# Attention and a gated feed-forward layer on one core: another table for the order of the steps and for the places of their tiles

## The chip, the core and the metric

The kernel runs on one core of a Trainium2 chip. The metric is the time of one execution on the device in microseconds (us), the median of several runs. Engines: PE is TensorE (its weight loads, PEld, run beside its matmuls), DVE is VectorE, ACT is ScalarE, POOL is GpSimd; SP issues nearly all transfers. Each engine works through its own queue in the written order and waits, where it must, for semaphores of other engines and of transfers.

## The reference

```python
k_all = concat([k_g, k_l]); v_all = concat([v_g, v_l])          # 8 batches, 8 heads, 32 + 512 rows, 64 columns
out_g = softmax(q_g @ k_all.T / 8) @ v_all                      # 32 global rows see all
s_l   = concat([q_l @ k_g.T, where(|i - j| <= 32, q_l @ k_l.T, -1e9)]) / 8
out_l = softmax(s_l) @ v_all                                    # 512 local rows see a band and the global rows
x  = concat([out_g, out_l]) as 4352 tokens x 512
xn = x / sqrt(mean(x * x) + 1e-6) * rms_g
g  = xn @ w_gate; v = xn @ w_val                                # 512 x 1536 each
y  = (g * sigmoid(g) * v) @ w_out                               # 1536 x 512
```

## The kernel before

The tokens come in nine chunks: chunk c of 0 to 7 holds the 512 local rows of batch c, chunk 8 the 256 global rows of all batches. While the feed-forward products of chunk c run, the attention of chunk c + 1 or c + 2 is done in pieces between them. Weights and tokens are split into a high and a low part in float16, and a product is three matmuls.

All steps are first only written down, under names, and then issued in the order of a table. `ORDER` (line 66) lists 3692 names as `chunk:step.part`; each engine's queue is what the list has for it, in the list's order, so moving a name moves all its instructions, transfers too. `PAGES` (line 391) gives each of 1169 larger tiles, in the order in which they are written down, one of 43 pages of 4 KB per partition (`a` to `d` are its quarters) or of 8 wider ones; `BANKS` (line 438) gives 444 PSUM tiles one of 8 banks. A tile that gets a place which another one had waits for that one's last reader. `JOBS` (line 40), which holds the steps of the first stage in their logical order, and all code stand as they are. The issuing loop is the last of the kernel:

```python
for name in ORDER.split() or list(plan):
    for call in plan.pop(name):
        call()
```

The first stage (the names that begin with `0:`) makes chunk 0's attention in four units of two heads (0 to 3) and chunk 1's in units 4 to 7, readies the weights, and does the feed-forward of chunk 0. Its steps, for a unit u:

- `Lu` loads queries and keys (256 and 384 KB), `Su` is 32 score products on PE (64 instructions), `Mu.h.g` adds the mask and takes the row's extreme on DVE (four for a half h), `Eu.h` is four exponentials on ACT, `Tu.h` four transposes on PE, `Cu.h` their copy out of PSUM on ACT, `Vu` loads the values (1 MB), `Au` is the product with them on PE (64 instructions), `Ru` and `Xu` divide on DVE, `Qu` squares on ACT and `Zu` sums on DVE.
- For a weight block i: `Wi` loads 1 MB, `mi`, `si`, `li` or `ki`, `gi` make it float32 (m and k on ACT, or m and l on DVE; s and g on DVE), `qi` sums squares on ACT, `ai` (ACT) and `di` (DVE) split it. `pg` sums a group's squares on PE and `eg` makes its scales on DVE. `z0` to `z6` handle the norm's gains.
- `N0.0` to `N0.12` are small DVE steps for the norm of chunk 0, `D0.j` its four diagonal matrices, `U0.k` the turn on PE (8 instructions each), `H0.k` (ACT) and `Y0.k` (DVE) the high and low parts.
- `If.wi` are the first feed-forward products of chunk 0 (6 matmuls of 512 columns), `B`, `b`, `h`, `c`, `r` what follows on ACT and DVE, `Oi.j` the second products.

From chunk 1 on, `c:Pk` and `c:Ok` are steps of a chunk's products, `c:Rk`, `c:tk`, `c:nk` what DVE, ACT and POOL do on them, `c:wk` transfers of weights, and `c:X/i+d` the attention steps of chunk c + d: `S` (scores, 128 PE instructions), `A` and `B` (values, 80 each), `GS`, `GT`, `GA` for the global rows.

Of the kernel before, what the change touches and what calls it, by code (L numbers as in the profile page):

```python
# [2327 lines left out]
```

## Time and profile before

| | us |
|---|---|
| median of 3 runs | 902.93 |
| lowest and highest | 902.28, 904.0 |
| the profiled execution | 904.84 |
| its span, first to last instruction | 903.1 |
| PE busy in the span | 869.2 |

The span is what the profile resolves; the profiled execution took 1.7 us more than it. PE is the busiest engine. A busy PE counts a matmul's pipelined end too, so beside the busy time the idle time in front of its instructions is to be read, with what ended it, and the TensorE clock that was granted.

### The profile page before, as it was taken

The page shows a single profiled execution, that of the slowest core. Times are in us where ns is not written, and L with a number is a line of the kernel's source. Part 1 is how long each engine was busy: PE and PEld are TensorE (multiplying, and loading weights), DVE is VectorE, ACT ScalarE, POOL GpSimd, SP SyncE. Part 2 cuts the span into 40 slices and gives each one's busy share as a digit, 9 for nine tenths or more (in the row PEclk, how much of TensorE's full clock was granted, in tenths as well). Part 3 has the DMA queues.
Part 4 walks back from the last instruction along what each step waited for, and adds up shares of the span by engine and source line. Part 5 has one row for each costly group of instructions (what it writes and reads, how often), then busy time and mean ns, then how long its engine had stood idle before and what let it go on. Part 6 is the DMA issues. An engine that isn't in the chain of part 4 may idle for free. (4 is left out here: it accounts for less than half of the span.)

```text
span 903.1 us, 27864 instructions
## 1 busy us (share of the span) xinstructions
PE 869.2 (96%) x11430; PEld 668.4 (74%) x11430; DVE 701.2 (78%) x1831; ACT 553.8 (61%) x1341; POOL 273.8 (30%) x244
## 2 busy tenths in 40 slices
...
DMA packets 101007, 212.04 MB, mean 235 GB/s; under 512 B 8080, under 2 KB 34448, under 8 KB 100880
## 3 DMA queue, kind: packets, MB, share of 16 engines
q1 hardware_dynamic: 100448, 209.94, 69.0%
q8 instruction: 89, 1.46, 0.7%
q10 hardware_dynamic: 432, 0.33, 0.1%
...
## 5 line engine op out<-in xcount | busy, mean ns | idle before, releaser
L2088 PE MATMUL bank<-page,page 128*128 128x256 f16 (+6 forms) x8212 | 714.6, 281 | 24.8 <-DMA page<-in_qk_dram 8.6
L2088 PEld LDWEIGHTS <-page 128*128 128x128 f16 (+1 forms) x5472 | 525.0, 98 | 175.5 <-issue 11.4
L2088 POOL TENSOR_TENSOR page<-page,page 128x512 f16<-128x512 f32 (+5 forms) x177 | 200.5, 1152 | 361.4 <-ACT page L2088 319.8
L2088 ACT CAST page<-page 128x512 f16<-128x512 f32 (+1 forms) x156 | 121.2, 797 | 93.4 <-DVE page L2088 72.5
L2088 ACT COPY page<-bank 128x512 f32<-128x512 f32 (+3 forms) x163 | 85.1, 543 | 115.7 <-PE bank L2088 103.1
L2088 DVE TENSOR_TENSOR page<-bank,page 128x512 f32<-128x512 f32 x155 | 104.7, 685 | 59.2 <-PE bank L2088 48.7
L2088 ACT ACTIVATE page<-page,sm 128x128 f32<-128x128 f32 x352 | 128.8, 389 | 24.4 <-DVE sm L2088 21.7
L2088 DVE TENSOR_TENSOR page<-page,page 128x256 f32<-128x256 f32 (+5 forms) x171 | 102.4, 609 | 11.0 <-ACT page L2088 8.7
L2088 PE MATMUL bank<-wide,page 32*64 32x96 f32 (+6 forms) x2268 | 103.5, 271 | 1.3 <-issue 1.3
L2088 POOL TENSOR_TENSOR page<-page,sm 128x512 f32<-128x512 f32 x24 | 27.9, 1176 | 214.4 <-DVE sm L2088 200.5
L2088 ACT ACTIVATE page<-page 128x512 f32<-128x512 f32 (+2 forms) x94 | 77.6, 894 | 10.2 <-DVE page L2088 5.5
L2088 PEld LDWEIGHTS bank<-page,page 64*32 64x32 f32 (+4 forms) x3232 | 58.4, 116 | 29.5 <-issue 14.7
L2088 DVE CUSTOM_DVE_ANT_0 page<-bank,page 128x128 f32<-128x128 f32 x256 | 62.0, 284 | 19.9 <-PE bank L2088 16.5
L2088 DVE TENSOR_TENSOR page<-page 128x256 f32<-128x256 f32 (+3 forms) x127 | 69.3, 556 | 1.2
L2088 DVE SCALAR_TENSOR_TENSOR page<-page,page 128x512 f32<-128x512 f32 x65 | 46.9, 734 | 12.6 <-ACT page L2088 12.4
L2088 DVE SCALAR_TENSOR_TENSOR page<-page,c_h,page 128x512 f32<-128x512 f32 x69 | 51.7, 769 | 0.9
L2088 ACT ACTIVATE page<-page,half_inv 128x512 f32<-128x512 f32 x65 | 44.6, 716 | 12.8 <-DVE page L2088 11.5
L2088 ACT ACTIVATION_READ_ACCUMULATOR page<-page,sm 128x1 f32 x256 | 48.0, 187 | 0.0
L2088 PE MATMUL bank<-page,wide 128*128 128x256 f16 x330 | 41.7, 273 | 0.6 <-ACT page L2088 0.6
L2088 ACT ACTIVATE page<-bank,half_inv 128x512 f32<-128x512 f32 (+1 forms) x36 | 21.7, 610 | 31.7 <-PE bank L2088 31.7
L2088 DVE STREAM_TRANSPOSE wide<-page 128x512 f32<-128x512 f32 x48 | 32.6, 696 | 6.5 <-POOL page L2088 6.5
L2088 PEld LDWEIGHTS <-wide 128*128 128x128 f16 x330 | 31.9, 98 | 5.1 <-issue 1.0
...
## 6 DMA issues: line engine op xcount, KB each, us to landing
page<-wd SPq DMA_DIRECT2D x113, 512.0 KB, 6.6
page<-wb SPq DMA_DIRECT2D x34, 512.0 KB, 7.2
page<-in_w_in_dram SPq DMA_DIRECT2D x24, 512.0 KB, 9.2
...
page<-wa SPq DMA_DIRECT2D x19, 512.0 KB, 6.0
...
page<-in_vw_dram SPq DMA_DIRECT2D x16, 512.0 KB, 8.9
```

Source lines behind the costliest of these rows:

```text
L2088: return lambda *a, **k: write(self.engine, lambda: call(*a, **k))
```

## The change

All three tables are replaced, `ORDER`, `PAGES` and `BANKS`; nothing else is. The names in `ORDER` are the same 3692, 118 of them at the same place in the list; 84 of 1169 pages and 57 of 444 banks are the same. No instruction is added or taken away. In the first stage the loads of units 0 and 1 come earlier (`L0` first, `L1` ahead of the weights), `T0` and the other steps of unit 0 come ahead of unit 2's, `E1` comes ahead of some of the work on weight blocks, and a step of `g2` stands between the `N0` and the `D0` steps. Later the changes are local: products of a chunk change places with each other and with the attention steps between them. The start of each table, and two later places of `ORDER`:

```diff
--- before
+++ after
 ORDER = """
-0:L2.0 0:L0.0 0:S0.0 0:M0.0.0 0:M0.0.3 0:M0.0.1 0:M0.0.2 0:E0.0.0 0:z0.0 0:M0.1.2 0:L3.0 0:W1.0
-0:W3.0 0:M0.1.3 0:M0.1.0 0:M0.1.1 0:S2.0 0:E0.1.0 0:M2.0.2 0:M2.1.1 0:M2.1.2 0:M2.0.0 0:L1.0
-0:M2.0.1 0:S3.0 0:M2.1.0 0:M2.0.3 0:M2.1.3 0:E2.1.0 0:E2.0.0 0:V0.0 0:z1.0 0:z2.0 0:M3.1.0 0:W0.0
-0:z2.1 0:z2.4 0:z2.5 0:M3.0.0 0:M3.0.1 0:z2.6 0:z3.0 0:M3.1.1 0:M3.1.3 0:M3.1.2 0:E3.1.0 0:M3.0.3
-0:m3.0 0:z4.1 0:M3.0.2 0:m1.1 0:m3.1 0:z2.2 0:T2.1.0 0:C2.1.0 0:T0.0.0 0:C0.0.0 0:z4.0 0:s3.0 0:z2.3
-0:E3.0.0 0:m1.0 0:T0.1.0 0:C0.1.0 0:T2.0.0 0:l1.1 0:s1.0 0:l1.0 0:S1.0 0:M1.0.0 0:M1.0.1 0:M1.0.2
-0:M1.0.3 0:E1.0.0 0:M1.1.3 0:M1.1.2 0:M1.1.0 0:M1.1.1 0:E1.1.0 0:g1.0 0:g1.1 0:V2.0 0:q1.0 0:V1.0
-0:R0.0 0:T3.1.0 0:V3.0 0:C2.0.0 0:T3.0.0 0:W2.0 0:A0.0 0:W4.0 0:m0.0 0:T1.0.0 0:T1.1.0 0:C3.0.0
-0:k3.0 0:L4.0 0:z4.2 0:m0.1 0:C3.1.0 0:l0.0 0:s0.0 0:C1.0.0 0:C1.1.0 0:X0.0 0:g0.0 0:W7.0 0:Q0.0
-0:A2.0 0:p1.0 0:l0.1 0:g0.1 0:q0.0 0:g3.0 0:g3.1 0:W5.0 0:R2.0 0:W8.0 0:X2.0 0:R3.0 0:e1.0 0:z5.0
-0:q3.0 0:z6.0 0:z6.1 0:z6.2 0:e1.1 0:A1.0 0:R1.0 0:X1.0 0:Q2.0 0:p0.0 0:e0.0 0:e1.2 0:e0.1 0:e0.3
-0:W6.0 0:Z2.0 0:e1.3 0:Q1.0 0:e0.2 0:A3.0 0:X3.0 0:a0.0 0:Z1.0 0:Q3.0 0:Z0.0 0:Z3.0 0:N0.0.0
-0:N0.1.0 0:N0.2.0 0:e0.4 0:N0.3.0 0:N0.4.0 0:N0.5.0 0:N0.6.0 0:N0.7.0 0:N0.8.0 0:N0.9.0 0:N0.10.0
-0:N0.11.0 0:N0.12.0 0:m2.0 0:s2.0 0:L5.0 0:D0.3 0:D0.2 0:k2.0 0:D0.1 0:D0.0 0:d0.0 0:m4.0 0:g2.1
-0:a1.0 0:U0.0.0 0:s4.0 0:U0.1.0 0:g2.0 0:W9.0 0:k4.0 0:m7.0 0:W11.0 0:H0.0.0 0:d1.0 0:g4.0 0:U0.3.0
-0:U0.2.0 0:Y0.0.0 0:q2.0 0:p2.0 0:H0.1.0 0:Y0.1.0 0:S4.0 0:H0.2.0 0:H0.3.0 0:e2.0 0:Y0.2.0 0:M4.0.0
...
+0:L0.0 0:S0.0 0:L2.0 0:S2.0 0:M0.0.2 0:M0.0.0 0:M0.0.1 0:z0.0 0:M0.0.3 0:M0.1.0 0:E0.0.0 0:M2.1.0
+0:M2.1.1 0:M2.1.2 0:M2.1.3 0:M0.1.2 0:L3.0 0:M2.0.2 0:E2.1.0 0:M0.1.1 0:M0.1.3 0:S3.0 0:M3.1.2
+0:z1.0 0:z2.0 0:M2.0.1 0:E0.1.0 0:M2.0.3 0:M2.0.0 0:E2.0.0 0:M3.0.3 0:M3.0.2 0:z2.1 0:M3.1.1
+0:M3.1.0 0:M3.1.3 0:E3.1.0 0:T0.0.0 0:C0.0.0 0:L1.0 0:M3.0.1 0:M3.0.0 0:E3.0.0 0:W1.0 0:V0.0 0:z2.4
+0:W0.0 0:m1.0 0:T0.1.0 0:T2.0.0 0:W3.0 0:z2.6 0:z2.5 0:l1.0 0:C2.0.0 0:m1.1 0:T2.1.0 0:C0.1.0 0:s1.0
+0:l1.1 0:g1.0 0:g1.1 0:q1.0 0:z3.0 0:z4.1 0:T3.1.0 0:z4.0 0:R0.0 0:S1.0 0:M1.0.3 0:M1.0.1 0:M1.0.0
+0:M1.0.2 0:V2.0 0:M1.1.1 0:M1.1.0 0:C2.1.0 0:M1.1.2 0:E1.0.0 0:M1.1.3 0:z4.2 0:R2.0 0:z2.2 0:m0.0
+0:m0.1 0:s0.0 0:A0.0 0:l0.0 0:m3.0 0:E1.1.0 0:g0.0 0:m3.1 0:k3.0 0:l0.1 0:T1.1.0 0:V1.0 0:T1.0.0
+0:p1.0 0:A2.0 0:s3.0 0:X0.0 0:g3.0 0:C1.0.0 0:Q0.0 0:g0.1 0:q0.0 0:T3.0.0 0:C1.1.0 0:g3.1 0:V3.0
+0:X2.0 0:z2.3 0:p0.0 0:e0.0 0:e0.1 0:e0.2 0:z5.0 0:C3.0.0 0:Q2.0 0:z6.0 0:W2.0 0:C3.1.0 0:e1.0
+0:q3.0 0:R3.0 0:A1.0 0:R1.0 0:Z0.0 0:e1.1 0:z6.1 0:W4.0 0:Z2.0 0:z6.2 0:X1.0 0:A3.0 0:a0.0 0:X3.0
+0:Q1.0 0:e1.2 0:L4.0 0:Z1.0 0:Q3.0 0:Z3.0 0:N0.0.0 0:N0.1.0 0:N0.2.0 0:N0.3.0 0:N0.4.0 0:N0.5.0
+0:N0.6.0 0:m2.0 0:s2.0 0:N0.7.0 0:k2.0 0:N0.8.0 0:N0.9.0 0:N0.10.0 0:N0.11.0 0:N0.12.0 0:g2.0 0:D0.1
+0:W7.0 0:a1.0 0:D0.2 0:D0.3 0:m4.0 0:W5.0 0:W6.0 0:D0.0 0:U0.3.0 0:U0.0.0 0:d0.0 0:g2.1 0:e0.3
+0:s4.0 0:U0.1.0 0:k4.0 0:d1.0 0:g4.0 0:q2.0 0:H0.1.0 0:U0.2.0 0:H0.0.0 0:g4.1 0:m7.1 0:S4.0 0:m5.0
+0:k5.0 0:Y0.1.0 0:q4.0 0:Y0.0.0 0:H0.3.0 0:e1.3 0:p2.0 0:m7.0 0:H0.2.0 0:M4.0.0 0:e2.0 0:M4.0.2
+0:e2.1 0:a2.0 0:m6.0 0:s7.0 0:s5.0 0:e0.4 0:g5.1 0:e2.3 0:k6.0 0:L5.0 0:g5.0 0:q5.0 0:Y0.3.0
+0:Y0.2.0 0:e0.5 0:W8.0 0:e1.4 0:l7.0 0:W12.0 0:I0.00.0 0:I1.00.0 0:l7.1 0:g7.0 0:g7.1 0:q7.0 0:m8.0
+0:W11.0 0:I0.10.0 0:d2.0 0:I1.10.0 0:a3.0 0:M4.1.3 0:I0.11.0 0:s6.0 0:I0.01.0 0:M4.1.2 0:I1.11.0
+0:g6.0 0:I1.01.0 0:g6.1 0:M4.1.1 0:p3.0 0:q6.0 0:B0.0 0:e3.0 0:m11.0 0:I2.00.0 0:W9.0 0:e2.4
+0:I2.01.0 0:l8.1 0:M4.0.3 0:e2.2 0:W10.0 0:B1.0 0:M4.1.0 0:e3.3 0:m9.0 0:M4.0.1 0:W17.0 0:e2.5
...
-2:P48.0 2:P49.0 2:P50.0 2:t37.1 2:t42.1 1:GX/1+1.1 2:w41.0 2:Y/2+1.1 2:t38.1 2:R41.2 2:t43.1
-2:S/0+2.0 2:P46.0 2:t44.0 2:X/2+1.3 2:t43.0 2:M1/0+2.1 2:t43.2 2:t44.1 2:N1/0+2.0 2:Y/2+1.2 2:P51.0
...
+2:w41.0 2:GX/1+1.0 2:GX/1+1.1 2:R41.2 2:t42.0 2:P49.0 2:X/2+1.0 1:R53.1 2:t42.1 2:t36.1 2:t43.0
+3:w13.0 2:t43.1 2:X/2+1.2 2:w44.0 2:P50.0 2:P51.0 2:t37.1 2:t38.1 2:t44.0 2:t45.0 2:X/2+1.3 2:P52.0
+2:Y/2+1.0 2:Y/2+1.2 2:P46.0 2:S/0+2.0 2:Y/2+1.3 2:n45.0 2:n45.1 2:M1/0+2.1 2:M0/0+2.0 2:N3/0+2.0
...
-5:R34.0 5:t35.0 5:t36.0 5:R34.1 5:t35.1 5:t36.1 5:w36.0 5:t19.0 5:P37.0 5:P38.0 5:B/2+1.0 5:w40.0
...
+5:P37.0 5:t35.1 5:R36.1 5:t36.0 5:t36.1 5:R36.0 5:P39.0 5:R39.0 5:B/2+1.0 5:V/0+2.0 5:O1.0 5:t37.0
...
 PAGES = """
-3a 0c 2a 0c 3c 10a 2a 10a 3c 13a 1a 16a 16a 0a 1a 4c 11a 12a 0a 24a 4a 5a 23a 10c 4a 6a 7a 14a 19a
...
+3a 0c 2a 0c 3c 10a 11a 4c 3c 13a 2a 7a 16a 0a 1a 4c 12a 6a 0a 24a 4a 5a 23a 10c 4a 7a 8a 5a 19a 20a
...
 BANKS = """
-0 1 3 2 0 4 1 2 3 2 1 0 1 0 4 1 3 1 0 4 5 0 2 1 4 4 2 0 1 2 0 5 4 1 3 6 3 7 5 5 6 4 0 4 3 7 1 5 1 3
...
+0 1 7 6 1 0 2 3 4 7 6 0 2 5 6 3 4 1 6 5 0 3 4 7 5 2 3 0 1 2 4 5 3 5 7 6 0 6 1 1 5 6 0 1 4 2 7 6 5 3
...
```

## Rows read from the trace of the kernel before

**Rows 1.** The page: busy time by engine, and the queue of instruction packets.
```profile
PE 869.2 (96%) x11430; PEld 668.4 (74%) x11430; DVE 701.2 (78%) x1831; ACT 553.8 (61%) x1341; POOL 273.8 (30%) x244
...
q8 instruction: 89, 1.46, 0.7%
```
**Rows 2.** Who PE waited for: us in total, times, longest us.
```profile
PE bank L2088 <- issue: 7.5, 8, 2.1
...
PE bank L2088 <- ACT page L2088: 4.1, 7, 0.9
```
**Rows 3.** Busy time by stretch: PE, PEld, DVE, ACT, POOL, granted clock, DMA share, GB/s.
```profile
26.80:36.90 10.10, 8.31 (x207) 7.34 (x210) 8.69 (x26) 9.48 (x17) 0.00 (x0) 0.50 1.03 406
...
40.40:47.10 6.70, 3.20 (x15) 3.20 (x16) 6.39 (x22) 6.70 (x9) 0.00 (x0) 0.50 1.02 401
47.20:51.00 3.80, 3.80 (x102) 3.51 (x101) 3.80 (x7) 3.21 (x6) 0.00 (x0) 1.00 0.84 276
51.00:160.00 109.00, 108.19 (x990) 55.09 (x989) 106.76 (x268) 94.49 (x190) 0.00 (x0) 1.00 0.50 172
160.00:903.00 743.00, 731.80 (x9758) 587.79 (x9756) 558.08 (x1411) 420.12 (x1044) 273.60 (x240) 1.00 0.71 235
```
**Rows 4.** Transfers issued at 1.18 (L2's keys), 2.11 (L0's), 12.68 (W0): us to landing.
```profile
page<-in_qk_dram SPq DMA_DIRECT2D x1, 384.0 KB, 4.4
...
page<-in_qk_dram SPq DMA_DIRECT2D x1, 384.0 KB, 6.4
...
page<-in_w_in_dram SPq DMA_DIRECT2D x1, 512.0 KB, 10.8
```
**Rows 5.** ACT in the first stage: start, length, instruction, idle before it.
```profile
11.00 0.40 ACT L2088 ACTIVATE page<-page,sm 128x128 f32<-128x128 f32 x1 [3.17 <-DVE sm L2088]
...
19.49 1.04 ACT L2088 COPY page<-bank 128x512 f32<-128x512 f32 x2
...
26.03 1.04 ACT L2088 ACTIVATE page<-page 128x1024 bf16<-128x1024 f32 x1
...
35.72 0.63 ACT L2088 ACTIVATE page<-page 128x512 f32<-128x512 f32 x1 [0.62 <-DVE page L2088]
```
**Rows 6.** PE in the first stage: A0 in two pieces, T1.1, A2, A3, U0, S4 with I0.00's first.
```profile
22.85 1.09 PE L2088 MATMUL bank<-page,page 128*32 128x64 f32 x63 [0.39 <-ACT page L2088]
26.07 0.22 PE L2088 MATMUL bank<-page,page 128*32 128x64 f32 x1 [2.13 <-issue]
...
27.69 1.11 PE L2088 MATMUL bank<-ident,page 128*128 128x128 f32 x4 [0.77 <-ACT page L2088]
28.73 1.94 PE L2088 MATMUL bank<-page,page 128*32 128x64 f32 x64
...
35.59 1.72 PE L2088 MATMUL bank<-page,page 128*32 128x64 f32 x64
43.90 5.39 PE L2088 MATMUL bank<-page,page 128*128 128x128 f32 x32 [6.59 <-DVE page L2088]
...
49.73 1.48 PE L2088 MATMUL bank<-page,page 64*32 64x128 f32 x65
```
**Rows 7.** DVE in the first stage: X3, N0.0, s2, the D0 steps, Y0.0 and Y0.1.
```profile
37.38 0.69 DVE L2088 TENSOR_TENSOR page<-bank,sm 128x512 f32<-128x512 f32 x1 [0.37 <-PE bank L2088]
...
39.89 0.17 DVE L2088 TENSOR_REDUCE rn<-ss 128x4 f32<-128x16 f32 x1
...
42.98 0.87 DVE L2088 TENSOR_SCALAR page<-ident,rn 128x128 f32<-128x128 f32 x4
...
46.22 0.75 DVE L2088 SCALAR_TENSOR_TENSOR page<-page,ends,page 128x512 int32<-128x512 int32 x1
...
49.08 1.41 DVE L2088 SCALAR_TENSOR_TENSOR page<-bank,gvec,page 128x512 f16<-128x512 f32 x2
```
**Rows 8.** PE later: the second pieces of S/0+2 in chunk 2 and B/2+1 in chunk 5.
```profile
352.09 0.86 PE L2088 MATMUL bank<-page,page 64*32 64x128 f32 x39 [0.44 <-issue]
...
636.16 0.44 PE L2088 MATMUL bank<-wide,page 32*64 32x64 f32 x26 [0.73 <-issue]
```

686 lines of the change are left out of this document (340 added, 346 removed), and 16 rows, old and new, of the table BANKS.

## The prediction

> **What bounds the kernel now.** I read the page first. PE is busy for 869.2 of the span's 903.1 us [rows 1], so what another order can give back lies in the 34 us in which PE idles. The waits of PE and the timeline split these by place. 8.6 us pass until the first keys have landed, and PE's sum of work has little in it until its queue reaches U0 at 43.90, after an idle stretch of 6.59 us [rows 6]. The table by stretch then shows two different regimes. From 51 to 160 us PE, DVE and ACT are all near full (108.2, 106.8 and 94.5 of 109 us); from 160 us on PE alone is (731.8 of 743) [rows 3]. From U0 to the last matmul PE idles for about 8.6 us in all, and most of it is no wait for data: "issue" ends 7.5 us in 8 waits, the longest of 2.1 at 26 us, so 5.4 us in 7 waits behind U0; ACT ends another 4.1 us, most of it ahead of U0 [rows 2, 6]. So two things carry the prediction: when the first feed-forward product (I0.00, at 50.8 us, the last 0.4 of the row that begins with S4 [rows 6]) can start, and what the seven later "issue" waits become. The work behind I0.00 is the same set of matmuls in both tables, and a moved start moves the end one to one, as long as DVE and ACT keep up.
>
> What "issue" is can be read from where it falls. PE has 22,860 instructions [rows 1] and the packet queue brought 89 packets of 16 KB, so one packet holds 256 of them. Counting PE's queue with its semaphore instructions, all eight waits begin 192 or 193 above a multiple of 256. They are waits for the next packet, and they fall where little time lies in the 256 instructions (128 pairs of weight load and matmul) before: inside A0, S/0+2, B/2+1 or just behind [rows 6, 8].
>
> **The first stage, step by step.** *The start.* L2's keys land at 1.18 + 4.4 = 5.6 us and L0's at 2.11 + 6.4 = 8.5; S0 waits for the latter [rows 4]. With L0 first, S0 starts 3.0 us earlier, and E0.0, which starts ACT's long chain at 11.00 [rows 5], at about 8.2 (M0.0.2, 0.2 us, now stands ahead of M0.0.0). *What is given back at once.* The new ACT queue has E2.1 second, behind S2 and L2, whose keys now land at 8.5; S2 takes 2.0, M2.1.0 0.3, so E2.1 starts at about 10.9, and ACT, which ends E0.0 (1.7 us) at 9.9, waits for 1.1 us. *The queue up to E1.1.* Before, ACT ran from 11.00 to 26.03 without a break [rows 5], to the end of E1.1. After, q1 (1.04) and C2.0 (half of 1.04) stand ahead of it too, and z0 (0.2) is done before: 8.2 + 1.1 + 15.0 + 1.0 + 0.5 - 0.2 = 25.6. So E1.1 ends only 0.4 us earlier; the rest of the gain is in what is already done by then.
>
> *PE up to A3.* A0 had 63 of its 64 instructions done in 1.09 us and then waited for 2.13 us for its packet [rows 6]. In the new queue T3.0 and T2 stand elsewhere, and the same count falls into T1.1, which waits for E1.1 anyway, over 3 us after A0; I take this wait at nothing, and if that cover is gone it is at most the 2.13 of before. From T1.1 at 25.7 PE then has T1.1 and T1.0 (1.11 and 0.85), p1 0.8, A2 1.94, T3.0 0.85, p0 0.8, z5 0.5, A1 1.93, A3 1.72 [rows 6], 10.5 us: A3 ends at 36.2, not 37.3, if these run at the 1.2 GHz that was granted before (0.50 in that stretch [rows 3]). ACT has C1.1, C3.0 and C3.1 done in time for it. X3, Q3 and Z3 follow (0.69, 0.63, 0.68), and N0.0 starts at about 38.3 instead of 39.89 [rows 7]. If PE, which has no gap in these 10.5 us now, is granted 2.4 GHz for the last three products, they take 1.09 each [rows 6], and N0.0 starts at 36.6, where ACT's own sum ends too.
>
> *From N0.0 to I0.00.* The N0 steps, s2 and the four D0 steps took 4.0 us; g2.0 (0.66 by its distance to the next) now stands among them, so U0 starts 4.6 behind N0.0: at 42.9, or 41.2 at best, where it was 43.90 [rows 6, 7]. From U0 to I0.00 it was 6.9 us: 5.39 for the 32 matmuls of U0, of which 3.3 at 1.2 GHz, the rest and S4 and p2 at 2.4 [rows 3, 6]. PE idles ahead of U0 after the change as well, so it starts there at 1.2 GHz again; all 32 at that level would be 1.7 us more. So I0.00 starts between 41.2 + 6.9 = 48.1 and 42.9 + 8.6 = 51.5, against 50.82: from -2.7 to +0.7 us. DVE's queue says the same: Y0.1 and Y0.0, the last that I0.00 needs, stand behind 11.0 us of work counted from N0.0 (10.2 before), so 47.7 to 49.4. I take -1.2, near the middle, since the fast end needs the clock twice.
>
> *Transfers and what hides them.* The first eight loads are the same set, so the eighth lands when it did, at 12.68 + 10.8 = 23.5 [rows 4]: that is W3 now instead of W0. k3, its first user on ACT, comes at 25.6; the cover is 2.1 us, and if it is gone all of ACT behind k3 waits one to one. The second half of W5 now waits in SP's queue for A3, W6 and W8 behind it too, and W11 for S4. Their blocks are wanted by ACT 4 us or more after they land; nothing in it at present. POOL has no step ahead of 160 us [rows 3].
>
> *Behind I0.00.* Counted with the durations of before, DVE and ACT have by each In, by T5.0 and by O0 the same work behind them as before within some 2 us, and the least lead of a product's inputs is 0.4 us or so in both orders (I4.00, p4 and I6.00 now; I0.00, T7.0 and O0.1 before). I take no change, from -0.7 (the small waits there all gone) to +1.5.
>
> **The packets behind U0.** I counted the same boundaries in the new queue of PE and summed the work in the 128 pairs ahead of each. From chunk 1 on 24 of 76 such stretches held less than 6.7 us of work before, and 22 do now. Of the seven waits, five have the same stretch before them within 0.1 us (4.6 us of work at P6 of chunk 1, for one). Two have more: for the one in S/0+2 of chunk 2 it is 10.8 us instead of 7.4, as three more product steps (P51, P52, P46) stand between B/2+1 and it, and for the one in B/2+1 of chunk 5 it is 7.3 instead of 6.1, with P39 ahead. These waits, 0.44 and 0.73 [rows 8], should go: -1.2. The bounds: all seven gone, -5.4; or as many again, since transfers are moved too and a packet's lateness depends on them, +5.4. I take -1.2 because the five others keep their places.
>
> The Trainium skill, "Runtime: NRT & Kernel Launch", section Instruction fetch mechanics, holds against this term: it has the refills in 16 KiB blocks of 256 instructions too, but calls the crossing of a block's boundary "mostly hidden". By that rule alone the seven waits would be something else, the packets' wait would be worth nothing, and the time would be the first rival's. The eight waits at one and the same count speak against it here.
>
> **Rest.** R, t and n steps of later chunks only change places; PE's idle time there that is not "issue" sums to about 3 us, and I keep it, from -1 to +3.
>
> **The sum** is made against the profiled execution (904.84, span 903.1) and carried over to the median, 902.93, as a difference: 902.93 - 1.2 - 1.2 = 900.5.
>
> **Rivals.** *The packets stay as late as before:* only the first stage gains, 902.93 - 1.2 = 901.7. For it: five of seven stretches are unchanged. Against: the two others are clearly longer. The rule of the Trainium skill named above ("Runtime: NRT & Kernel Launch", Instruction fetch mechanics) gives this time too, by taking the whole term out. *The clock takes the first stage's gain:* U0 runs at 1.2 GHz throughout, I0.00 starts at 50.8 or later, and the packets are as before: 902.9, to 903.6. For it: before, the level rose 3.3 us after U0's first matmul, and nothing in the order makes it do so again. Against: ACT and DVE are earlier in any case. This one is also that the change does nothing that can be measured. *Slower: more late packets.* The place is the bursts of small matmuls (S, A, B) in chunks 1 to 6, where a stretch of less than 7 us meets full transfer rings. Twice as many waits of the mean length, 5.4/7 = 0.77, would be 5.4 more; less the first stage's 1.2 that is 907.1. It decides when the later waits come to 8.4 us (5.4 + 1.2 + 1.8), eleven of them. For it: new short stretches in front of B/0+2 in chunks 2 and 4, P24 in chunk 6. Against: as many others grew.
>
> **How the numbers follow.** The forecast has 0.45, at 900.5 with its own range from 898.3 to 902; the first rival 0.25 at 901.7; the second 0.15 at 902.9; the slower one 0.15 at 907. About 0.2%, 1.8 us, is what a measurement of this kernel can tell from no change. Faster by more than that (under 901.1) are most of the forecast and a third of the first rival: 0.48; within it the rest of these and the second rival: 0.37; slower (over 904.7) the last: 0.15. The range leaves out the better bounds of both terms taken together and the far part of the slower case: 897.8 to 904.6.
>
> **What would show it.** Right: S0 at 5.6 to 5.8, E0.0 near 8.2, a wait of ACT for DVE near 10 us, A0 without a break, U0 at 41 to 43 and I0.00 at 48 to 50.5; "issue" at 4 to 5 us behind U0, none in S/0+2 of chunk 2 or B/2+1 of chunk 5. Wrong: S0 that still waits past 8 us, W3 landing behind ACT's turn for k3, a new wait of PE for q6 at p4 or for DVE at I4.00 and I6.00, or more than ten "issue" waits. If U0 starts early and I0.00 doesn't, it was the clock.

## The result, and the profile after

The kernel after takes 895.1 us (median of 893.34 to 896.85), where the kernel before, run beside it, takes 902.71: a ratio of 0.9913 with a 95% interval from 0.9886 to 0.9941. Against the 902.93 from which the forecast was made that is 7.8 us, where 2.4 were forecast (900.5), and outside the range, whose lower end was 897.8. The direction was right and the size was not. The profiled execution of after took 896.6 us with a span of 894.8 (before: 904.84 and 903.1), so the profiled gain is 8.3.

The page of after answers [rows 1]: busy time by engine, and the packet queue. The work is the same, the span is shorter.

```profile
PE 866.1 (97%) x11430; PEld 665.6 (74%) x11430; DVE 705.4 (79%) x1831; ACT 551.1 (62%) x1341; POOL 271.6 (30%) x244
...
q8 instruction: 89, 1.46, 0.7%
```

Whom PE waited for in after (us in total, times, longest), against [rows 2]: "issue" fell from 7.5 us in 8 waits to 3.0 in 3, and ACT is now named for the long wait ahead of U.

```profile
PE bank L2088 <- ACT page L2088: 13.0, 6, 7.4
...
PE bank L2088 <- issue: 3.0, 3, 1.7
```

PE's timeline of after through the first stage (start, length, form, idle time before it and its releaser), against [rows 6]. The rows are A0's second part, T1.1 with T1.0, A2, A1 with A3, the 32 matmuls of U0 with S4 behind them, and I0.00.

```profile
20.37 0.99 PE L2088 MATMUL bank<-page,page 128*32 128x64 f32 x56 [1.56 <-ACT page L2088]
23.82 2.48 PE L2088 MATMUL bank<-ident,page 128*128 128x128 f32 x8 [2.46 <-ACT page L2088]
...
26.66 1.93 PE L2088 MATMUL bank<-page,page 128*32 128x64 f32 x64
...
30.52 2.14 PE L2088 MATMUL bank<-page,page 128*32 128x64 f32 x128
40.09 6.51 PE L2088 MATMUL bank<-page,page 128*128 128x128 f32 x96 [7.43 <-ACT page L2088]
...
47.17 1.02 PE L2088 MATMUL bank<-page,page 128*128 128x512 f16 x4
```

A3 ends at 32.66 where it ended at 37.31, U0 starts at 40.09 instead of 43.90, I0.00 at 47.17 instead of 50.82. So 3.65 of the 8.3 us are there when the first feed-forward product starts. From I0.00 to the start of the third matmul from the end it was 848.25 us before and is 843.64 after: another 4.61.

DVE in after, against [rows 7]: N0.0, the four D0 steps, and Y0.1 with Y0.0. N0.0 is 4.44 us earlier, and U0 follows it after 4.64 us, as forecast (4.6).

```profile
35.45 0.17 DVE L2088 TENSOR_REDUCE rn<-ss 128x4 f32<-128x16 f32 x1
...
39.07 0.87 DVE L2088 TENSOR_SCALAR page<-ident,rn 128x128 f32<-128x128 f32 x4
...
45.38 1.41 DVE L2088 SCALAR_TENSOR_TENSOR page<-bank,gvec,page 128x512 f16<-128x512 f32 x2
```

The table by stretch of after, columns as in [rows 3]: in the stretch that holds A2 to A3 the mean granted clock is 0.84 instead of 0.50. It counts the idle time behind A3 too; from 26.6 to 30.5 us, up to the end of z5, it is 0.59, and from 30.5 to 32.7, for A1 and A3, 1.00. Behind 160 us PE is busy for 726.4 us where it was 731.8, but 27 matmuls fewer lie there, since the start is earlier. Over the same 10,746 matmuls, those from I0.00 on, PE is busy for 838.0 us after and 840.2 before.

```profile
26.80:36.90 10.10, 5.86 (x208) 5.01 (x204) 8.58 (x30) 10.10 (x18) 0.00 (x0) 0.84 1.03 405
...
160.00:903.00 743.00, 726.44 (x9731) 584.65 (x9729) 560.47 (x1411) 416.13 (x1041) 271.41 (x240) 1.00 0.71 237
```

### The profile page after: what moved, and what is told of

It is laid out like the page before. It is cut to its first block, busy times and chain, and to the rows that moved or that the text cites. A ratio compares the mean times of both kernels' runs of the same rounds, so it can differ in the third digit from the quotient of the medians.

```text
span 894.8 us, 27793 instructions
## 1 busy us (share of the span) xinstructions
PE 866.1 (97%) x11430; PEld 665.6 (74%) x11430; DVE 705.4 (79%) x1831; ACT 551.1 (62%) x1341; POOL 271.6 (30%) x244
## 4 chain that ended last, share of the span: by engine, by line
PE 88%; DVE 4%; ACT 1%; issue 1%; DVEq 0%; ACTq 0%
PE bank L2088 88%; DVE page L2088 4%; ACT page L2088 1%; DVE wide L2088 0%; DVE xg L2088 0%; DVE ws L2088 0%; DVE hs L2088 0%; DVE sm L2088 0%; DVE pow L2088 0%; DVE half_inv L2088 0%; DVE gsm L2088 0%; DVE c_h L2088 0%; DVEq L2088 0%; DVE nt L2088 0%; ACTq L2088 0%
## 5 line engine op out<-in xcount | busy, mean ns | idle before, releaser
L2088 PE MATMUL bank<-page,page 128*128 128x256 f16 (+6 forms) x8226 | 726.0, 279 | 19.9 <-ACT page L2088 9.0
L2088 PEld LDWEIGHTS <-page 128*128 128x128 f16 (+1 forms) x5340 | 512.4, 98 | 164.8 <-issue 10.4
L2088 POOL TENSOR_TENSOR page<-page,page 128x512 f16<-128x512 f32 (+5 forms) x155 | 175.5, 1150 | 302.8 <-ACT page L2088 279.2
L2088 ACT CAST page<-page 128x512 f16<-128x512 f32 (+1 forms) x142 | 108.1, 784 | 69.0 <-DVE page L2088 55.2
L2088 DVE TENSOR_TENSOR page<-page,page 128x256 f32<-128x256 f32 (+4 forms) x159 | 97.1, 626 | 10.1 <-ACT page L2088 8.0
L2088 PEld LDWEIGHTS bank<-page,page 64*32 64x32 f32 (+4 forms) x3120 | 55.2, 112 | 25.0 <-ACT page L2088 10.8
L2088 PE MATMUL bank<-wide,page 32*64 32x96 f32 (+6 forms) x2042 | 62.4, 267 | 0.9 <-issue 0.9
L2088 DVE TENSOR_TENSOR page<-page 128x256 f32<-128x256 f32 (+3 forms) x116 | 60.1, 532 | 1.2 <-PE bank L2088 0.2
L2088 PE MATMUL bank<-page,wide 128*128 128x256 f16 (+2 forms) x496 | 60.9, 276 | 0.0
L2088 PEld LDWEIGHTS <-wide 128*128 128x128 f16 x462 | 44.7, 98 | 13.6 <-issue 0.8
L2088 POOL TENSOR_TENSOR wide<-page,wide 128x512 f16<-128x512 f32 (+2 forms) x23 | 25.0, 1098 | 42.1 <-ACT wide L2088 42.1
```

Of the source, the lines that this page charges most:

```text
L2088: return lambda *a, **k: write(self.engine, lambda: call(*a, **k))
```

## The experiments

The runs are in one table, but for two misses that stand further down (b_move, b_L0move). Ratio is against runs of the kernel before on the same chip. S0, A3, U0 and I0.00 are starts in the profile of the run (U0: the first of its four groups); "packets" is the sum of PE's packet waits behind U0, and "rest" the time from I0.00 to the start of the third matmul from the end. Kernels that begin with b_ are the kernel before with an edit, those with a_ the kernel after.

| run | ratio, interval | S0 | A3 | U0 | I0.00 | packets | rest |
|---|---|---|---|---|---|---|---|
| before | 1 | 8.63 | 35.59 | 43.90 | 50.82 | 5.4 | 848.3 |
| b_again | 0.9994 [0.9981, 1.0007] | 7.95 | 34.98 | 43.49 | 51.50 | 2.3 | 844.9 |
| b_L0 | 0.9978 [0.9967, 0.9990] | 5.94 | 33.74 | 42.25 | 49.59 | 3.5 | 845.9 |
| b_bank | 1.0014 [1.0003, 1.0025] | 7.92 | 35.68 | 44.18 | 52.19 | 3.2 | 846.1 |
| b_bank2 | 0.9983 [0.9970, 0.9996] | 7.96 | 33.54 | 42.05 | 49.61 | 2.7 | 846.3 |
| b_warm | 1.0025 [1.0011, 1.0040] | 7.75 | 34.09 | 42.33 | 50.43 | 5.4 | 849.8 |
| b_warm128 | 0.9991 [0.9982, 1.0001] | 7.99 | 34.59 | 43.86 | 49.73 | 2.2 | 846.4 |
| b_move2 | 0.9967 [0.9955, 0.9980] | 8.27 | 35.18 | 43.69 | 51.20 | 2.4 | 843.9 |
| b_all | 0.9966 [0.9953, 0.9980] | 5.86 | 34.13 | 42.63 | 49.58 | 0.5 | 842.7 |
| b_all2 | 0.9935 [0.9916, 0.9954] | 6.05 | 32.79 | 41.30 | 49.01 | 1.2 | 843.7 |
| b_shift64 | 1.0290 [1.0264, 1.0316] | 8.23 | 35.47 | 43.98 | 51.98 | 20.8 | 872.8 |
| after | 0.9913 [0.9886, 0.9941] | 6.17 | 31.55 | 40.09 | 47.17 | 3.0 | 843.6 |
| a_again | 0.9918 [0.9905, 0.9932] | 5.70 | 31.47 | 40.00 | 48.22 | 0.5 | 841.9 |
| a_L2 | 0.9927 [0.9911, 0.9943] | 7.84 | 33.24 | 41.78 | 50.21 | 0.6 | 842.0 |
| a_move | 0.9903 [0.9885, 0.9922] | 6.01 | 31.40 | 39.94 | 46.92 | 0.0 | 840.9 |
| a_warm | 0.9915 [0.9902, 0.9929] | 6.76 | 33.17 | 41.98 | 48.66 | 0.1 | 841.6 |
| a_warm2 | 0.9911 [0.9897, 0.9925] | 5.89 | 31.35 | 40.46 | 45.92 | 0.4 | 842.9 |
| a_best | 0.9916 [0.9899, 0.9934] | 6.06 | 31.48 | 42.29 | 47.75 | 0.0 | 843.2 |

(In a_warm2 and a_best I0.00 itself is earlier than what PE is fed with, so their "rest" is not comparable.)

**The start, alone and taken back (b_L0, a_L2).** One load changes its place in the order.

```diff
-0:L2.0 0:L0.0 0:S0.0 ...      (b_L0, from the kernel before)
+0:L0.0 0:L2.0 0:S0.0 ...
-0:L0.0 0:S0.0 0:L2.0 ...      (a_L2, from the kernel after)
+0:L2.0 0:L0.0 0:S0.0 ...
```

> The kernel before with one edit: the load 0:L0.0 stands ahead of 0:L2.0, as in the kernel after; all else stays. Theory 1 (the one on record: the start of the first loads sets the first stage): 0:S0.0 comes at about 6.2 us instead of 8.63, E0.0 at 8.8 instead of 11.00, and I0.00 about 1.2 to 2.4 us sooner than 50.82; 901.5 us or less where the kernel before takes 902.7. Theory 2 (in the kernel before the line that sets the end of the stage is TensorE's own, from A0 on, at 1.2 GHz and with a packet wait of 2.13 us; S1 waits for the load of 0:L1.0, which this edit doesn't move): the early lead is used up in ScalarE's wait ahead of E1.0 (22.70 before), and I0.00 comes 0 to 0.5 us sooner; 902.2 to 902.9 us.

> The kernel after with that one edit undone: 0:L2.0 ahead of 0:L0.0. In the kernel after ScalarE works without a gap from 8.81 to 43.37 us, and A3 starts at 31.55, right when ScalarE's C3.1 ends (31.50). Theory 1 and theory 2 both say that here the start counts: S0 at about 8.6, E0.0 at 11.0, the whole line of ScalarE 2.0 to 2.4 us later, I0.00 at 49.2 to 49.6 instead of 47.17, and 897.1 to 897.5 us where the kernel after takes 895.1. The rival (the start is hidden and the clock alone gave the first stage) says 895.1 and I0.00 at 47.2 to 47.7.

b_L0 moved S0 by 2.0 to 2.7 us, U0 by 1.2 to 1.65 and I0.00 by 1.2 to 1.9 (against the two profiles of the kernel before), with a ratio of 0.9978, so 2.0 us. That is theory 1, the one on record; theory 2, that the lead is used up in a wait for L1, fell. a_L2 lost 1.8 us at A3 and at U0 against a_again, and 0.8 to 1.3 us of time (0.9927 against 0.9918 and 0.9913, intervals that overlap), less than the 2.0 to 2.4 expected; so here the trace shows the start's worth and the time alone does not. The start is worth about 1.5 us at U0 in both orders, near what the prediction gave the whole first stage (1.2). So the rest of the first stage has another source: a_L2 keeps the late start and still has U0 at 41.78, 1.7 to 2.1 us ahead of the kernel before.

**The clock alone (b_warm, b_warm128).** Matmuls into an unused bank fill TensorE's idle stretches.

```diff
+ ahead of T1.1: 3 x matmul(bank6[:, :256], ones, ones)      (b_warm, b_warm128)
+ ahead of p1:   4 x matmul(bank6[:, :256], ones, ones)
+ ahead of U0.0: 121 x matmul(bank6[:, :64], ones, ones)     (b_warm128 only)
```

> The kernel before with seven more matmuls (128x128 by 256 columns, into a bank that nobody reads) in two idle stretches of TensorE: three ahead of T1.1 (idle 0.77 us) and four ahead of p1 (idle 0.88 us). They do no work for the result. If the clock granted to A1 and A3 hangs on how busy TensorE was just before, A1 and A3 run at 2.4 GHz (1.1 us each instead of 1.94 and 1.72), A3 ends about 1.7 us sooner (35.6 instead of 37.31), and I0.00 comes 1.0 to 1.7 us sooner; 901.0 to 901.9 us. If the clock hangs on something else, the seven matmuls are idle time filled: no step moves by more than 0.2 us and the time stays at 902.7.

> The kernel before with matmuls that do no work for the result: three ahead of T1.1 and four ahead of p1 (by 256 columns), as before, and 121 more pairs (by 64 columns) in TensorE's idle time of 6.59 us ahead of U0.0. Together they are one packet, so that behind U0.0 every packet ends where it does in the kernel before. If a good part of the first stage's gain is the granted clock alone: A3 ends 0.7 to 1.5 us sooner against S0, U0.0 to U0.2 take 1.06 us each, I0.00 comes 2 to 3 us sooner than 50.82 (at 47.8 to 48.8), and the time is 899.7 to 901.2 us where the kernel before takes 902.7. If the order alone gave it: I0.00 at 50.0 to 50.8, and 902 to 902.9 us.

In b_warm the clock rose from 31.0 to 34.4 us, A1 took 1.4 us instead of 1.9, and A3 started 0.9 us ahead of b_again; but then U0 to U0.2 ran at 1.2 GHz throughout, and I0.00 was back at 50.43. Its ratio of 1.0025 comes from later: seven pairs more shift every packet's end by seven pairs, and the waits ahead of 1:P5, 2:P17 and in chunk 5 became 1.62, 1.56 and 1.91 us. b_warm128, in which the packets end as before, has the clock at 2.4 GHz under U0 (0.98 in the row below, columns as in [rows 3]); U0 to I0.00 took 5.87 us instead of 6.92 in before and 8.01 in b_again. But a packet wait of 1.91 us among the extra matmuls made U0 no earlier than before, and what was left, 0.6 to 0.8 us, can't be told from nothing. The clock under U0 is worth 1 to 2 us of TensorE's time, and it isn't what the change gains: its own U0 starts at 1.2 GHz.

```profile
43.80:49.00 5.20, 5.20 (x114) 5.18 (x116) 5.20 (x9) 5.20 (x8) 0.00 (x0) 0.98 0.96 353
```

**The PSUM places (b_bank, b_bank2).** Only entries of the table BANKS change.

```diff
- t11: 1   p1's sums: 2   a2: 0   a1: 0     (kernel before)
+ t11: 6   p1's sums: 7   a2: 0   a1: 0     (b_bank)
+ t11: 6   p1's sums: 5   a2: 7   a1: 6     (b_bank2)
```

> The kernel before with two PSUM places changed and nothing else: T1.1's products go to bank 6 instead of 1, p1's sums to bank 7 instead of 2 (both free until 49 us). If TensorE's line from A0 to A3 is held up by these places: T1.1 follows T1.0 without its 0.77 us of idle time, p1 follows A2 without its 0.88, A1 starts when ScalarE's C1.1 ends (32.0 instead of 33.0), A3 ends 1 us sooner, 1.7 if the clock rises for it too, and I0.00 comes 0.5 to 1.7 us sooner; 901.2 to 902.4 us where the kernel before takes 902.8. Rival (ScalarE and VectorE hold up the stage anyway): U0.0 moves by less than 0.3 us and the time stays at 902.8.

> The kernel before with four PSUM places changed: T1.1's products in bank 6 instead of 1, p1's sums in 5 instead of 2, a2 in 7 instead of 0, a1 in 6 instead of 0; no order changes. If the reuse of bank 0 holds up TensorE: A2 starts behind T1.1 at 27.1 to 27.3 (28.05 in the last profile of the kernel before) and no longer behind X0, A1 at 31.3 to 31.5, behind ScalarE's C1.1, instead of 32.4 behind X2, A3 ends 1.0 to 1.8 us sooner (35.1 to 35.9 instead of 36.9), U0.0 comes at 41.8 to 42.5 instead of 43.49, and the time is 901.0 to 902.2 where the kernel before takes 902.9. Rival (VectorE's order holds X1 and X3, and so N0, where they are): U0.0 within 0.4 us of 43.49, 902.5 to 903.3.

b_bank did not do what was expected. T1.1 came earlier (26.22 instead of 27.00 in b_again) and p1 too (29.60 instead of 30.88), but A2 and A1 stayed at 28.00 and 32.38. In the middle of A1 a packet wait of 0.57 us is new, and A3 and U0 came 0.7 us later than in b_again; the ratio of 1.0014 says slower by 1.3 us [0.3 to 2.3].

PE of b_bank: A2, A1 in two pieces.

```profile
28.00 1.67 PE L2080 MATMUL bank<-page,page 128*32 128x64 f32 x64 [0.73 <-ACT page L2080]
...
32.38 1.21 PE L2080 MATMUL bank<-page,page 128*32 128x64 f32 x42 [1.89 <-ACT page L2080]
34.16 0.86 PE L2080 MATMUL bank<-page,page 128*32 128x64 f32 x22 [0.57 <-issue]
```

The profile names ACT for the two waits, but ACT's copies for A2 and A1 had ended by 27.40 and 31.24; A2 and A1 start 0.1 us behind the ends of X0 and X2 on DVE (27.91 and 32.28). It is the same in b_again, where A2 starts at 28.05 and A1 at 32.39 on PE, and on DVE the two TENSOR_TENSORs X0 and X2, which read the products of A0 and of A2, end at 27.96 and 32.33. a0, a2 and a1 all lie in bank 0.

PE of b_again: A2, A1, A3, U0.

```profile
28.05 1.94 PE L2088 MATMUL bank<-page,page 128*32 128x64 f32 x64
...
32.39 1.93 PE L2088 MATMUL bank<-page,page 128*32 128x64 f32 x64 [0.20 <-DVE page L2088]
...
34.98 1.93 PE L2088 MATMUL bank<-page,page 128*32 128x64 f32 x64
43.49 4.85 PE L2088 MATMUL bank<-page,page 128*128 128x128 f32 x21 [6.58 <-DVE page L2088]
```

DVE of b_again: X0 and X2.

```profile
27.28 0.68 DVE L2088 TENSOR_TENSOR page<-bank,sm 128x512 f32<-128x512 f32 x1
...
31.64 0.69 DVE L2088 TENSOR_TENSOR page<-bank,sm 128x512 f32<-128x512 f32 x1
```

With banks of their own (b_bank2, PE: T1.0 with T1.1, A2, A1, A3, U0), A2 starts at 27.02, ahead of X0's end, and A1 at 31.32, released by ACT, each where it was expected:

```profile
25.84 1.09 PE L2080 MATMUL bank<-ident,page 128*128 128x128 f32 x8
27.02 1.10 PE L2080 MATMUL bank<-page,page 128*32 128x64 f32 x64
...
31.32 1.18 PE L2080 MATMUL bank<-page,page 128*32 128x64 f32 x64 [2.37 <-ACT page L2080]
...
33.54 1.94 PE L2080 MATMUL bank<-page,page 128*32 128x64 f32 x64
42.05 6.02 PE L2080 MATMUL bank<-page,page 128*128 128x128 f32 x32 [6.58 <-DVE page L2080]
```

U0 comes 1.44 us ahead of b_again's, and the time fell by 0.17%, 1.5 us [0.4 to 2.7]. In the table of after a0, a2, a1 and a3 have the banks 0, 3, 6 and 5. That is the place part of the change, and the profile of before hid it: A2 followed T1.1 without idle time on PE there [rows 6], since T1.1 itself had been held up until then by the same kind of reuse (t11 in the bank that C2.0 still read).

**Where the packets end (b_shift64).** Sixty-four pairs go ahead of 1:P0.

```diff
+ ahead of 1:P0: 64 x matmul(bank7[:, :64], ones, ones)
```

> The kernel before with 64 more pairs of weight load and matmul (128x128 by 64 columns, into the bank that 1:P0 writes next) ahead of 1:P0; they do no work for the result and take 1.7 to 3.5 us. From there on every instruction packet ends 64 pairs sooner in the order, so that the packets' ends fall into other places of the bursts of short matmuls: by the times of the kernel before, the shortest stretches between two ends become 1.5 us instead of 3.6, and 18 instead of 10 of them are under 6.2 us. Theory (a packet's wait is its transfer's lateness plus some 2.5 us, less the time that the stretch takes): 20 to 50 us more of waits where the count is 192 or 193 over a multiple of 256, so 925 to 955 us. Rival (where the packets end matters little, since the next is fetched while the last runs): 904.5 to 907 us.

929.11 us, 26 more than before. PE's waits (columns as above) and the longest one, in B/0+1 of chunk 2:

```profile
PE bank L2088 <- issue: 23.1, 10, 5.5
```
```profile
298.90 0.43 PE L2088 MATMUL bank<-wide,page 32*64 32x32 f32 x7 [5.47 <-issue]
```

All ten stand at a count of 192 or 193 over a multiple of 256, nine of them at new places behind 1:P0 (20.8 us), and the rival, that it matters little where the packets end, fell. The waits are not the whole price. PE is also busy for 10.8 us longer behind I0.00 than in the six profiles named below (850.7 against 839.9 on the mean), and only 2.0 of it are the 64 pairs. Around the five longest waits (1.96 to 5.47 us) the granted clock fell to 0.50 for some us; around the other four (1.1 to 1.5 us) it stayed at 1.00. Two of the five stretches, columns as in [rows 3]:

```profile
247.50:250.80 3.30, 3.30 (x106) 2.67 (x112) 0.00 (x0) 0.00 (x0) 3.22 (x4) 0.50 1.10 369
...
551.30:558.00 6.70, 6.05 (x35) 4.36 (x35) 1.75 (x4) 1.69 (x4) 3.01 (x3) 0.50 0.06 22
```

**The same kernels once more (a_again, b_again).**

> The kernel after, unchanged, profiled once more. If the lateness of a packet is fixed by the order of the work, the same three packet waits (ahead of 3:P13, 3:B/2+1, 5:O11; 3.0 us in sum) stand at the same instructions within 0.2 us each. If it changes from one execution to the next, some are gone and others come, always where the count of TensorE's instructions is 192 or 193 over a multiple of 256, and the time of a step behind I0.00 can be read from one profile to 1 or 2 us only. 895.1 us either way.

> The kernel before, unchanged, profiled once more. If packet waits are settled by where the packets end and which transfers are under way, five or more of the seven waits behind U0 come again at the same instructions, with lengths that differ by up to 0.7 us, and their sum is 3 to 6 us.

Waits of a_again and of b_again:

```profile
PE bank L2088 <- issue: 0.4, 1, 0.4
```
```profile
PE bank L2088 <- issue: 4.2, 5, 2.1
```

Of after's three waits one came again, inside O11 of chunk 5, with 0.37 us instead of 1.69 (first row: after, second: a_again):

```profile
642.36 1.03 PE L2088 MATMUL bank<-page,page 128*128 128x256 f16 x8 [1.69 <-issue]
```
```profile
641.39 1.03 PE L2088 MATMUL bank<-page,page 128*128 128x256 f16 x8 [0.37 <-issue]
```

In b_again the ones ahead of 1:P6, 1:S/0+2, 2:P17, 3:S/0+2 and 5:O10 came again (0.81, 0.75, 0.16, 0.35, 0.09), those in 2:S/0+2 and 5:B/2+1 did not. A place is where a wait can be; its length changes from one execution to the next, by up to 1.3 us, and so 5.4 us of packet waits in one profile was too much by about half. In b_again they sum to 2.3 us, below the 3 to 6 expected. The six profiles of kernels whose packets end as in before (before, b_again, b_L0, b_bank, b_bank2, b_warm128) have a mean of 3.2 us behind U0, the four with the packets of after (after, a_again, a_L2, a_warm) 1.1. I0.00 differs from profile to profile as well: 50.82 and 51.50 in the kernel before, 47.17 and 48.22 in the one after, so the first stage's gain is 2.6 to 4.3 us by which two are compared.

**Transfers out of a late packet's way (a_move, b_move2).** Transfers that stood in the queues when a late packet was asked for are written later, PE's order stays.

```diff
 a_move:  3:w42 -> behind 3:w31; 3:w27 -> behind 3:w50; 3:w55 4:w3 -> behind 3:V/0+2
          6:w24 6:w36 6:w32 7:w25 6:w48 -> behind 6:w11
 b_move2: 2:L/2+1 -> behind 1:w29; 3:w6 -> behind 2:w58
          4:w6 4:w32 -> behind 3:w40; 5:w53 5:w60 -> behind 6:w36
```

> The kernel after with nine transfers of the sync queue written later: 3:w42 behind 3:w31 and 3:w27 behind 3:w50; 3:w55 and 4:w3 behind 3:V/0+2; 6:w24, 6:w36, 6:w32, 7:w25 and 6:w48 behind 6:w11. No instruction of TensorE moves, so every instruction packet ends at the same instruction as in the kernel after. The theory that a packet's transfer comes late where it stands behind other transfers says that the three packet waits of the kernel after (0.44 us ahead of 3:P13, 0.87 ahead of 3:B/2+1, 1.69 ahead of 5:O11) go or shrink to under 0.4 us in sum, and 892.0 to 893.0 us where the kernel after takes 895.1. The rival, that these waits come from the instructions between the packet ends alone, leaves them at 3.0 us in sum and the time at 895.1.

> The kernel before with six transfers written later: 2:L/2+1 behind 1:w29, 3:w6 behind 2:w58, 4:w6 and 4:w32 behind 3:w40, 5:w53 and 5:w60 behind 6:w36 (2:w25 stays where it was). Theory of late packets: the waits ahead of 2:P17 and 5:O10 go, those ahead of 1:S/0+2 and 3:S/0+2 shrink or go, no transfer is waited for instead, and the time falls by 1 to 3 us, to 899.8 to 901.8 where the kernel before takes 902.8. Rival: 902.3 to 903.3.

b_move2 took 0.33% off the kernel before, 3.0 us [1.8 to 4.1], with PE's order untouched. Of its four targets the waits in 2:P17 and 5:O10 are gone, the one ahead of 1:S/0+2 is 0.20, the one in 3:S/0+2 is 1.07 and not shorter. So the order of transfers alone is worth this time; that all of it is packet waits isn't shown. In its one profile the rest is 2.4 us under the mean of the six, and of this 0.9 is packet waits, 0.9 other idle time of PE and 0.6 its busy time. On the packets the traces show one relation. Take the time from the start of a packet's transfer to the moment PE reaches its first instruction. In all the runs here, every packet wait has 2.2 to 2.9 us of it, and nothing over 3 us waits (67 packets got by without a wait at 2.2 to 3 us); a packet's transfer in turn starts between 4.7 us ahead of and 6.3 us behind the moment when PE begins the packet before it. In before the packets at 1:S/0+2, 2:P17 and 3:S/0+2 started 5.0, 3.9 and 4.1 us behind it; at the same counts in after it is 2.7, 2.1 and 1.1, and none waits, though PE has hardly more work between (6.7, 5.5 and 4.8 us against 7.0, 5.4 and 5.7 without the wait).

a_move has no packet wait at all behind U0 in its profile, and its rest of 840.9 us is the shortest; but a_again has only 0.5 us of them, so against after's usual execution there was little to take, and the ratio of 0.9903 can't be told from after's 0.9913.

**A miss (b_move, b_L0move).** The same edit with 2:w25 also written later.

> The kernel before with seven transfers of the sync queue written later: 2:L/2+1 behind 1:w29; 3:w6 and 2:w25 behind 2:w58; 4:w6 and 4:w32 behind 3:w40; 5:w53 and 5:w60 behind 6:w36. TensorE's order stays. If late packet transfers are what the kernel after saves behind I0.00, then the waits ahead of 1:S/0+2 (0.72 to 0.93 us in the profiles so far), 2:P17 (0.68 to 1.56), 3:S/0+2 (0.19 to 0.97) and 5:O10 (0.57 to 0.64) go or shrink to under a third, the one ahead of 1:P6 (1.1) stays, and the time falls by 1.5 to 3 us, to 899.7 to 901.2 where the kernel before takes 902.7. Rival (these waits are made up elsewhere, or their lateness comes from something other than the transfers under way): 902.3 to 902.9.

> The two edits of the kernel before together: 0:L0.0 ahead of 0:L2.0, and the seven transfers later. If the start and the packets add up: 1.8 to 2 us for the start and 1.5 to 3 for the packets, 897.7 to 899.4 us; what is then left to the 895.1 of the kernel after (2.6 to 4.3 us) belongs to the written order of the first stage. If they are one and the same gain: 900.7 to 901.5.

Both became slower (908.4 and 906.8 us; 1.0054 and 1.0044): 2:w25 loads the blocks of 2:P35 in the same chunk, and PE waited for it.

```profile
318.17 1.04 PE L2072 MATMUL bank<-page,page 128*128 128x256 f16 x4 [5.26 <-DMA page<-wd]
```

They say nothing on the packets' worth in time; b_move2 and the next pair replace them.

**The named parts together (b_all, b_all2).** L0 ahead of L2 and b_move2's transfers, with the two places of b_bank or the four of b_bank2.

> The kernel before with 0:L0.0 ahead of 0:L2.0, the two PSUM places and the six transfers together. If the three parts add up: 1.8 us for the start, 0.5 to 1.7 for the places, 1 to 3 for the packets, so 896.3 to 899.5 us; then most of what the change gives has a name. If the written order itself is needed: 899.5 to 901.5.

> The kernel before with 0:L0.0 ahead of 0:L2.0, these four places and the six later transfers. If the parts add up (1.8 us for the start, 0.7 to 1.9 for the places, 2.4 for the transfers): 896.8 to 898.2 us. If the places give nothing: 898.6 to 900.3, as in the run with the first two places.

b_all2 comes to 0.9935 [0.9916, 0.9954], 5.9 us of the 7.8 with no step of a compute engine moved, inside what the sum of the parts said. b_all, with the two places that don't help, is at 0.9966, outside its 896.3 to 899.5 us and no better than b_move2 by itself (0.9967): the start's 2.0 us do not show there. Its profile, at 898.1 us, is the fastest of its eleven runs and has the packet wait inside A1 again (0.29). What b_all2 lacks at U0 is 1.2 to 1.3 us, and the tables by stretch show where it lies: A1, p0 and A3 in b_all2 (first row), A1 and A3 in after (second).

```profile
30.10:34.70 4.60, 4.57 (x138) 4.17 (x138) 4.04 (x18) 4.54 (x8) 0.00 (x0) 0.50 1.03 405
```
```profile
30.50:32.70 2.20, 2.15 (x129) 1.88 (x129) 2.13 (x13) 2.20 (x6) 0.00 (x0) 1.00 1.03 410
```

In b_all2 PE idles 2.34 us ahead of A1 (for ACT) and runs A1 and A3 at 1.2 GHz; in after T3.0, p0 and z5 stand in that gap, PE has no idle time from 23.82 on, and A1 and A3 run at 2.4. That is the part of the written order. It is read from these two rows and was not tried alone, and neither were the new pages or the later moves of products.

**A better version? (a_warm, a_warm2, a_best).** TensorE's idle time ahead of U0 is filled in the kernel after, and Y0.1 and Y0.0 go ahead of other work on DVE.

```diff
+ ahead of U0.3: 128 x matmul(bank2[:, :100], ones, ones)      (all three)
- ... 0:d1.0 0:g4.0 ... 0:g4.1 0:m7.1 ... 0:Y0.1.0 0:q4.0 0:Y0.0.0
+ ... 0:d1.0 ... 0:Y0.1.0 0:Y0.0.0 0:g4.0 0:g4.1 0:m7.1 0:q4.0  (a_warm2, a_best)
+ transfers as in a_move                                        (a_best)
```

> The kernel after with 128 more pairs (128x128 by 100 columns, into the bank that U0.0 writes later) in TensorE's idle time of 7.43 us between A3 and U0.3; 128 pairs are just one packet, so all packets behind them end at the same instructions as in the kernel after. They do no work for the result. If the granted clock follows how busy TensorE was, U0.3 to U0.2 run at 2.4 GHz (4 groups of 1.06 us instead of 5.4 us for all), U ends at 44.3 to 44.5 instead of 45.51, and I0.00 comes only 0 to 0.4 us sooner than 47.17, since VectorE's Y0.0 (46.79 in the kernel after, behind g4.0, g4.1 and m7.1) is then what it waits for; 894.7 to 895.1 us. If the clock doesn't follow it, nothing moves by more than 0.1 us.

> The same 128 pairs, and VectorE's Y0.1 and Y0.0 ahead of g4.0, g4.1 and m7.1 (and ScalarE's q4, which needs g4, behind them in the written order, its place on its own engine kept). Y0.0 then ends at 45.0 to 45.5 and I0.00 comes at 45.9 to 46.1 instead of 47.17, which with nothing taken back later gives 894.0 us where the kernel after takes 895.1; the waits of p4 (0.52) and S5 (0.71) may take the lead back, then 894.9.

> The kernel after with all three edits that seemed to help: the nine transfers later, the 128 pairs ahead of U0.3, and VectorE's Y0.1 and Y0.0 ahead of g4. I0.00 at 45.9 instead of 47.17, but 0.5 us of it lost at I0.11 and 0.6 at S5 as they were with the last two edits alone; packet waits behind I0.00 under 0.4 us in sum where they are 0.5 to 3.0 in the profiles of the kernel after. 893.0 to 894.3 us where the kernel after takes 895.1; 895.1 if the lead is lost inside chunk 0 and the packet waits were rare anyway.

a_warm2's I0.00 came at 45.92, as expected, with U0 at 2.4 GHz (clock 1.00 in 40.0 to 45.5 us, where a_again has 0.50):

```profile
36.23 4.40 PE L2186 MATMUL bank<-ones 128*128 128x100 bf16 x96 [2.25 <-issue]
40.46 4.89 PE L2071 MATMUL bank<-page,page 128*128 128x128 f32 x96
...
45.92 1.24 PE L2071 MATMUL bank<-page,page 128*128 128x512 f16 x5
```

And little of it was left: 1:P0 started at 161.28 us, against 161.37 in after and 162.24 in a_again. PE waited for DVE instead, 0.5 us at I0.11 and 1.3 at S5 (0.7 in after); DVE is busy for 105.4 of the 109 us from 51 to 160 in after. None of the three differs from after by more than its interval, so no version here beats it.

## Why the prediction fell short, step by step

*What bounds the kernel, and the counting of packets*: right in the main. Most of the gain is in PE's idle time ahead of I0.00 and in packet waits (2.0 us are in PE's busy time, see below), and all waits named "issue" stand at the counts given.

*The start*: right (S0 at 6.17 for 5.6 to 5.8, E0.0 at 8.81 for 8.2), and the 1.2 us that the prediction gave the whole first stage at I0.00 is what this one edit gave in b_L0 (1.2 to 1.9). *ACT's wait of 1.1 us ahead of E2.1*: wrong. E2.1 began at 10.36, straight behind E0.0 in ACT's timeline, since S2 ran at 8.21 right behind S0:

```profile
8.81 0.41 ACT L2088 ACTIVATE page<-page,sm 128x128 f32<-128x128 f32 x1 [0.92 <-PE bank L2088]
...
10.36 0.39 ACT L2088 ACTIVATE page<-page,sm 128x128 f32<-128x128 f32 x1
```

But E1.1 ended at 25.15 instead of 25.6 only: E0.0 started 0.6 late.

*PE up to A3* is the first step that failed: 36.2 was taken, 32.66 measured. Two terms of the sum were mis-sized. T1.1 was charged with its whole 1.11 us behind E1.1, though each of its four transposes needs one exp of four: it ended at 25.44, not 26.8, which is 1.4 us (0.45 of it E1.1's earlier end). And the groups behind it were charged with the durations of before, 9.4 us; they took 7.2. Of these 2.2 us A1 and A3 are 1.5 (2.14 for 3.65), which ran at 2.4 GHz. The prediction had this as its better bound (N0.0 at 36.6) and saw that PE would have no gap, yet chose the other end, because 0.50 was granted before. It didn't ask why that was. PE had idle time there before, behind bank 0, t11's bank and p1's, and the new places and order take these away; a step without idle time ahead of it in the rows [rows 6] was taken for one that nothing held up. The places alone did not bring the clock: A3 took 1.94 us in b_bank2 and 1.93 in b_all2. The bound itself was too high as well: N0.0 came at 35.45, and three products at 1.09 us in the prediction's own sum give 36.0 by PE, not 36.6.

*From N0.0 to I0.00*: right, 4.64 us to U0 and 7.08 from there (6.9 to 8.6 was given). *Transfers*: right; k3 began at 25.06, right behind E1.1, so W3 was no wait. *Behind I0.00, DVE and ACT*: right in size; PE's idle time behind 52 us that isn't a packet's is 3.1 us after and 3.2 before, at other places.

*The packets behind U0* is the second step that failed. The count of boundaries was right, the two waits named as gone are gone, and the five that "keep their places" mostly aren't there: only the one in chunk 5 (O10, now O11) is. The stretch of work ahead of a boundary is half of the matter. The other half, how late the packet's own transfer starts, was named as a bound of 5.4 us and then set to "no change"; in after it is 1.8 to 4.6 us earlier at six of the seven boundaries. The time from I0.00 on fell by 4.0 us on the mean of the profiles in the groups above (846.3 and 842.3), where 1.2 was forecast. Moving transfers alone gave b_move2 a rest of 843.9. Packet waits themselves account for 2.1 of the 4.0 (3.2 and 1.1). Other waits account for none: PE's other idle time from I0.00 on is 3.7 us in the six profiles and 3.8 in the four. What remains is PE's busy time over the same matmuls, 839.9 and 837.9. A wait adds a little to it (1:P6 took 2.54 us with its wait of 1.09 and 1.29 without it, 0.16 more than the wait), but most of these 2.0 us has no shown cause.

*The rivals*: all three predicted too little or the wrong sign. The second (the clock takes the first stage's gain) has one thing right: U0 does start at 1.2 GHz again. The Trainium skill's rule behind the first ("Runtime: NRT & Kernel Launch", Instruction fetch mechanics: the crossing of a block "mostly hidden") agrees with the count, 10 of 90 packets waited for even in b_shift64, and not with the price, 23.1 us there. *The range* missed because it took the better bounds of both terms together for unlikely. The first came and went further (3.65 us for 2.7). The second did not come as such, as packet waits fell by 2.4 us between the two first profiles and not by 5.4; with PE's shorter busy time it was 4.6 from I0.00 on.
